# One planned list of steps replaced by another: attention and a gated unit on one core

## The chip, the core and the metric

The kernel runs on one core of a Trainium2 chip. The core has five engines, each with its own queue of instructions that it works through in order: TensorE (PE; its weight loads are PEld), VectorE (DVE), ScalarE (ACT), GpSimd (POOL) and SyncE (SP), which here only issues transfers. ScalarE and GpSimd issue some transfers too. The metric is the time of one execution in microseconds of device time, the median of several runs.

## The reference

For 8 batches of 8 heads, 576 tokens and 64 columns a head, all float32:

```python
kv = np.einsum('bhsd,bhse->bhde', k, v)
out = np.einsum('bhsd,bhde->bhse', q, kv)
rms = np.sqrt(np.mean(out * out, axis=-1, keepdims=True) + 1e-06)
x = out / rms * g_norm              # then heads side by side: (8, 576, 512)
gate_pre = sum over 5 taps of conv_w[tap] * x shifted by 4 - tap tokens
gate = 1 / (1 + np.exp(-gate_pre))
result = (gate * (x @ w_val)) @ w_out
```

w_val, conv_w and w_out come as 512 x 512, 5 x 512 and 512 x 512 arrays of 8-byte floats, which the kernel turns into 4-byte ones by itself.

## The kernel before

The kernel is a list of steps. PLAN (line 19) is a text of 1242 steps, each a name with its arguments and, behind an @, the numbers of the rooms that it takes. The loop at line 882 goes through the list and calls the function of each step, which records its instructions. Every engine's queue therefore holds its instructions in the order of the list, and a step waits where its inputs or its room are not ready; what stands behind it on the same engine waits too. A room is one of a few fixed buffers (line 274): 8 banks of PSUM, 4 of "ot" (output rows), 4 of "gate", 3 of "w64" (staged weights and token sums), 3 of "sq", 3 of "x", one each of k0, k1, v0 and v1 and so on.

For a batch b the steps are these:

- load_half (line 339) loads one half of k or v, 576 KB; load_q (350) loads a pair of heads' rows of q with four transfers into one of three places of qs. All of them are on SP's queue but for a few of batch 0.
- kv_product (467, TensorE, 72 small matmuls) makes k^T v for half of the heads, kv_copy (487, ScalarE) copies it, turn_q (496, VectorE) transposes one load_q.
- raw_pair and raw_tail (566, 569, recorded at line 550) multiply q by kv, for two chunks of 128 tokens or for the last 64. square (582, ScalarE), sums (603, VectorE), powers (612, GpSimd, the root) and normalise (619, ScalarE, eight operations at line 635) make x. For four of the five chunks turn_blocks (659, VectorE) and move_blocks (663, two transfers on SP and two on GpSimd) transpose it, for the last one turn_x and keep_x (644, 650) do; halo (672, GpSimd) shifts the first rows.
- gate_start (677, ScalarE), four gate_taps (683, VectorE, line 685), gate_end (690, ScalarE, the sigmoid at line 692) and gated (708, VectorE, line 710) make one of four blocks of the gate and multiply it in.
- Batches 0 and 1 multiply x by w_val with val_product (694, TensorE) and keep_val. From batch 2 on the product is done in seven smaller ones in place of eight: x_sums (722, VectorE), val_fast (733, TensorE, line 746) and val_keep (750, ScalarE or VectorE).
- Two batches together are an output group i. token_sums (802, VectorE), fast_product (818, TensorE, line 837) and fast_keep (841) multiply by w_out in the same manner, out_product (771, line 784) and keep_out do the last 64 tokens of both. store (865, line 869) issues four transfers of 64 KB on SP's queue, store_last (862) the last rows, two on SP and two on ScalarE.

At the start q of batches 0 and 1 is turned by TensorE (turn_q_rows, 507, and sort_q, 523), and the weights are narrowed: stage_weight (439) loads a quarter of w_val or w_out (512 KB, SP's queue) and narrow_weight has eight parts for it, numbered 0, 5, 6, 4, 7 on VectorE (lines 399, 416, 421, 411, 425) and 1, 2, 3 on ScalarE. Part 4 is the last that reads the staged quarter and so frees its w64 room. val_product reads a column block of w_val after part 7 of it.

The order in the list is a planner's, written out; the kernel holds nothing of the planner. Steps of different batches are woven together: while batch b is multiplied by w_val, batch b + 1 is normalised and the output group before is multiplied by w_out.

Of the kernel before, what the change touches and what calls it, by code (L numbers as in the profile page):

```python
# [22 lines left out]
turn_q_rows 0 3 @ 4; sort_q 0 2; turn_q_rows 0 0 @ 5; sort_q 0 3; start_warm 3 256 @ 6; load_q_rows 1 1;  # L23
sort_q 0 1; load_q_rows 1 0; stage_weight wval 2; kv_product 0 0 @ 7 0; sort_q 0 0; load_half v 1 1;
narrow_weight cw 0 0 @ 0; load_half k 1 1; kv_half 0 0; raw_half 0 3 0 @ 2; narrow_weight cw 0 1;
narrow_weight cw 0 2; kv_product 0 1; stage_weight wval 3; narrow_weight cw 0 3; stage_weight wout 0 @ 1;
narrow_weight cw 0 4; narrow_weight wval 0 0 @ 1; raw_half 0 0 0 @ 3; stage_weight wout 1 @ 2; kv_half 0 1;
narrow_weight cw 0 5 @ 0; narrow_weight cw 0 6 @ 1; raw_half 0 2 0 @ 4; narrow_weight cw 0 7;
narrow_weight wval 0 1; raw_half 0 3 1; narrow_weight wval 0 5 @ 2; raw_half 0 0 1; narrow_weight wval 0 6 @ 3;
square 0 3 @ 0; raw_half 0 4 1 @ 6; square 0 0 @ 1; turn_cw @ 1; sums 0 3 @ 0 0; raw_half 0 2 1;  # L30
narrow_weight wval 0 2; raw_half 0 4 0; powers 0 3; narrow_weight wval 1 0 @ 0; keep_cw; load_half v 1 0;
square 0 2 @ 2; raw_half 0 1 0 @ 5; sums 0 0; square 0 4 @ 0; narrow_weight wval 0 3;
narrow_weight wval 1 5 @ 0; raw_half 0 1 1; sums 0 4; start_warm 1 256 @ 0; narrow_weight wval 1 1;
load_half k 1 0; sums 0 2; square 0 1 @ 1; narrow_weight wval 0 4; powers 0 2; narrow_weight wval 1 2;
sums 0 1; load_half v 2 0 @ 0; turn_q_rows 1 3 @ 7; narrow_weight wval 1 3; normalise 0 3 @ 0;
turn_q_rows 1 0 @ 1; sort_q 1 3 @ 1; narrow_weight wval 0 7; turn_x 0 3 @ 0; load_q 2 2;
narrow_weight wval 2 0 @ 1; turn_q_rows 1 1 @ 2; narrow_weight wval 1 6 @ 1; powers 0 1; keep_x 0 3;
normalise 0 4 @ 1; turn_q_rows 1 4 @ 7; normalise 0 2 @ 2; narrow_weight wval 2 1; turn_x 0 4 @ 6;
narrow_weight wval 1 4; keep_x 0 4; turn_x 0 2 @ 0; narrow_weight wval 2 2; narrow_weight wval 2 5 @ 2;
kv_product 1 1 @ 4 6; narrow_weight wval 1 7; keep_x 0 2; narrow_weight wval 2 3; narrow_weight wval 2 6 @ 3;  # L40
val_product 0 1 1 @ 0; sort_q 1 1; narrow_weight wval 3 0 @ 0; halo 0; normalise 0 0 @ 0; load_half k 2 1 @ 0;
normalise 0 1 @ 1; sort_q 1 4; turn_x 0 0 @ 3; narrow_weight wval 3 5 @ 0; narrow_weight wval 2 4;
turn_x 0 1 @ 2; narrow_weight wval 3 1; stage_weight wout 3 @ 0; val_product 0 0 1 @ 5;
narrow_weight wout 0 5 @ 1; keep_x 0 0; narrow_weight wout 1 5 @ 2; narrow_weight wval 2 7; keep_x 0 1;
narrow_weight wval 3 2; narrow_weight wout 1 6 @ 3; val_product 0 0 0 @ 7; narrow_weight wout 0 0 @ 1;
narrow_weight wval 3 3; narrow_weight wout 0 6 @ 2; gate_start 0 0 @ 0; narrow_weight wval 3 6 @ 1; sort_q 1 0;
narrow_weight wval 3 4; kv_product 1 0; gate_tap 0 0 3; gate_start 0 3 @ 1; narrow_weight wval 3 7;
turn_q_rows 1 2 @ 3; narrow_weight wout 1 0 @ 0; gate_start 0 1 @ 2; val_product 0 3 0 @ 2; gate_tap 0 0 2;
load_q 2 1; kv_copy 1 1; kv_copy 1 0; sort_q 1 2; gate_tap 0 3 3; gate_tap 0 0 1; raw_tail 1 @ 6 1; load_q 2 0;
gate_tap 0 3 2; keep_val 0 0 0; raw_pair 1 3 @ 3 4; keep_val 0 0 1; square 1 4 @ 0; gate_tap 0 1 3;  # L50
keep_val 0 3 0; raw_pair 1 1 @ 5 7; gate_start 0 2 @ 3; gate_tap 0 0 0; square 1 3 @ 2; val_product 0 1 0 @ 2;
sums 1 4 @ 1 1; keep_val 0 1 1; gate_tap 0 1 2; load_half k 2 0 @ 0; square 1 2 @ 1; powers 1 4;
narrow_weight wout 1 1; sums 1 3; load_half v 2 1 @ 0; square 1 1 @ 0; gate_tap 0 1 1; powers 1 3;
val_product 0 2 0 @ 0; narrow_weight wout 1 2; narrow_weight wout 3 5 @ 0; gate_tap 0 2 3; normalise 1 4 @ 2;
sums 1 2; narrow_weight wout 1 3; turn_q 2 2 @ 0; turn_x 1 4 @ 1; normalise 1 3 @ 0; powers 1 2;
# [5 lines left out]
load_half k 3 1 @ 0; narrow_weight wout 0 3; gate_tap 0 3 1; kv_copy 2 0; powers 1 1; normalise 1 0 @ 2;  # L61
val_sums 1; val_product 1 1 1 @ 6; narrow_weight wout 0 4; gate_tap 0 3 0; gate_end 0 0; halo 1; kv_copy 2 1;
# [3 lines left out]
sums 2 0 @ 0 0; val_product 1 0 1 @ 6; narrow_weight wout 2 1; weight_sums 0; keep_x 1 1; powers 2 0;  # L66
load_q 3 0; narrow_weight wout 3 0 @ 0; gate_end 0 2; gated 0 0; square 2 1 @ 2; val_product 1 3 0 @ 1;
gated 0 2; narrow_weight wout 3 1; sums 2 1; square 2 3 @ 0; load_half v 3 1 @ 0; narrow_weight wout 2 5 @ 0;
narrow_weight wout 3 2; turn_q 3 2 @ 1; val_product 1 2 0 @ 0; gate_start 1 2 @ 2; sums 2 3; square 2 2 @ 1;
load_half v 3 0 @ 0; narrow_weight wout 2 6 @ 2; narrow_weight wout 3 3; powers 2 3; load_half k 3 0 @ 0;  # L70
gate_tap 1 2 3; narrow_weight wout 2 2; val_product 1 1 0 @ 2; sums 2 2; keep_val 1 3 0;
narrow_weight wout 2 3; turn_q 3 1; gate_end 0 3; powers 2 2; narrow_weight wout 2 4; val_product 1 2 1 @ 1;
keep_val 1 0 1; keep_val 1 1 0; token_sums 0 0 2 @ 1; keep_val 1 2 0; gate_start 1 0 @ 0;
narrow_weight wout 3 4; normalise 2 3 @ 1; gated 0 3; powers 2 1; val_product 1 0 0 @ 6; turn_q 3 0;
narrow_weight wout 3 7; keep_val 1 2 1; load_q 3 3; normalise 2 2 @ 2; narrow_weight wout 2 7;
fast_product 0 1 0 @ 2; gate_tap 1 0 3; kv_product 3 1 @ 1 0; token_sums 0 0 0 @ 2; fast_keep 0 1 0 @ 3;
load_q 4 0; keep_val 1 0 0; normalise 2 0 @ 0; turn_blocks 2 2; fast_product 0 0 0 @ 5; weight_sums 1;
weight_sums 2; fast_product 0 0 1 @ 7; normalise 2 1 @ 2; turn_blocks 2 3; fast_product 0 0 3; turn_blocks 2 0;
kv_product 3 0; token_sums 0 0 1; fast_keep 0 0 0 @ 0; fast_keep 0 0 1 @ 1; gate_start 1 1 @ 3;
turn_blocks 2 1; raw_tail 2 @ 6 3; val_sums 3; fast_product 0 1 1 @ 4; move_blocks 2 3; square 2 4 @ 2;  # L80
token_sums 0 0 3; move_blocks 2 1; sums 2 4; fast_product 0 1 2; fast_keep 0 1 1 @ 2; gate_tap 1 0 2;
move_blocks 2 0; fast_product 0 0 2; turn_q 3 3; fast_keep 0 1 2; gate_start 1 3 @ 1; fast_product 0 0 5;
gate_tap 1 0 1; kv_copy 3 1; fast_keep 0 0 2; powers 2 4; move_blocks 2 2; kv_copy 3 0; gate_tap 1 3 3;
fast_product 0 1 4; load_half v 4 1 @ 0; weight_sums 3; fast_product 0 0 4; normalise 2 4 @ 1; gate_tap 1 1 3;
raw_pair 3 1 @ 0 1; gate_tap 1 0 0; load_q 4 2; fast_keep 0 0 4; raw_pair 3 3 @ 3 6; gate_tap 1 3 2;
square 3 1 @ 0; fast_keep 0 1 4; fast_product 0 0 6; square 3 3 @ 1; sums 3 1 @ 1 1; square 3 0 @ 2;
fast_keep 0 0 5; fast_product 0 1 6; powers 3 1; load_q 4 1; square 3 2 @ 0; gate_tap 1 2 2; gate_end 1 0;
# [829 lines left out]
```

## Time and profile before

| | |
|---|---|
| median of 3 runs | 299.33 us (298.89 to 300.11) |
| the profiled execution | 300.76 us |
| its span, first to last instruction | 299.0 us |
| granted TensorE clock, mean | 0.996 |
| TensorE matmuls, weight loads | 287.7 us, 225.3 us busy |
| VectorE, ScalarE, GpSimd | 270.1, 198.4, 119.2 us busy |
| transfers | 55.51 MB, mean 186 GB/s |
| instruction queue q8 | 26 packets, 0.43 MB |

The span is the time from the first instruction to the last. "Busy" is the time in which an engine has at least one instruction at work. A row of waits reads: who waited, the line of its instruction, for whom, total us, number of waits, the longest. A row of the chain or of the timeline begins with the start and the length in us. The name behind a DMA wait is that of a transfer that shares the semaphore with the awaited one, which need not be the same transfer. A step's times follow from the trace, because each engine's instructions stand there in the list's order. q8 is taken to bring TensorE's program, which is by far the longest: its packets come all through the span, and 0.43 MB over TensorE's 2 x 3279 instructions are 65 bytes for each.

### The profile page before, as it was taken

To read this page: it belongs to the slowest core of one execution; us is meant where nothing else is said; L and a number is where in the kernel's file an instruction comes from. 1 tells how busy PE (TensorE), PEld (TensorE's weight loads), DVE (VectorE), ACT (ScalarE), POOL (GpSimd) and SP (SyncE) were. 2 spreads that over 40 slices of the span, in tenths; PEclk is the share of its full clock that TensorE was granted. 3 is DMA by queue.
4 is the path that set the end of the run, shared out by engine and by line. 5 is a ranking of instruction groups with operands and counts; after the bars stand their busy time and mean duration, and the time that the engine had idled before them with its cause. 6 is when DMAs were issued, how large, how long until landed. Compare 5 with 4: busy or idle time off the path is not lost.

```text
span 299.0 us, 8649 instructions
## 1 busy us (share of the span) xinstructions
PE 287.7 (96%) x3279; PEld 225.3 (75%) x3279; DVE 270.1 (90%) x483; ACT 198.4 (66%) x621; POOL 119.2 (40%) x131
## 2 busy tenths in 40 slices
PE   7988999999999999899999999999999999999994
PEld 3766787878887868678887757888887588788583
DVE  1699999999999999979999999999999998999812
ACT  1899999999685868664389386757477654614230
POOL 3056054663667049610494287040494072000020
PEclk9999999999999999999999999999999999999998
DMA  7999984787599556976979389654551063130244
GB/s 268 381 389 409 269 246 122 235 256 230 139 235 268 182 152 150 277 181 215 259 171 311 85 202 330 171 148 114 136 146 39 21 147 80 49 94 0 74 121 123
DMA packets 32009, 55.51 MB, mean 186 GB/s; under 512 B 6166, under 2 KB 14358, under 8 KB 31968
## 3 DMA queue, kind: packets, MB, share of 16 engines
q1 hardware_dynamic: 29328, 49.50, 56.2%
q0 software_dynamic: 1760, 3.43, 5.2%
q10 hardware_dynamic: 880, 2.03, 1.9%
q8 instruction: 26, 0.43, 0.6%
q14 instruction: 15, 0.12, 0.1%
HBM read 39.21 MB, written 9.44 MB: 163 GB/s over the span
## 4 chain that ended last, share of the span: by engine, by line
PE 57%; DVE 23%; DMA 7%; ACT 4%; POOL 3%; issue 3%; SPq 2%; DVEq 0%; ACTq 0%
PE bank L746 21%; PE bank L837 19%; DVE gate L685 7%; PE bank L475 4%; PE bank L697 4%; PE bank L550 4%; PE bank L784 4%; DMA qs<-in_q_dram 4%; POOL rt L616 2%; DVE xs L731 2%; DMA k<-in_k_dram 2%; DVE ot L847 2%; DVE ss L606 2%; DVE y L660 1%; PE bank L562 1%
## 5 line engine op out<-in xcount | busy, mean ns | idle before, releaser
L685 DVE SCALAR_TENSOR_TENSOR gate<-xT,cwT,gate 128x576 f32<-128x576 f32 x128 | 100.0, 806 | 0.3
L616 POOL TENSOR_TENSOR rt<-ss,mhalf 128x8 f32<-128x8 f32 (+3 forms) x38 | 71.0, 1887 | 57.2 <-DVE ss L606 56.8
L635 ACT ACTIVATE x<-bank,rt 128x64 f32<-128x64 f32 x252 | 56.5, 398 | 2.8 <-POOL rt L616 2.4
L668 POOL DMA_DIRECT2D xT<-y x48 | 26.6, 559 | 71.7 <-issue 27.8
L837 PE MATMUL bank<-wsum,w 128*128 128x256 f32 x192 | 46.8, 381 | 0.0
L837 PEld LDWEIGHTS bank<-wsum,w 128*128 128x128 f32 x192 | 36.0, 190 | 6.6 <-issue 0.8
L746 PE MATMUL bank<-xs,vsum 128*128 128x288 f32 x144 | 38.2, 409 | 0.2 <-DVE xs L731 0.2
L746 PEld LDWEIGHTS bank<-xs,vsum 128*128 128x128 f32 x144 | 26.9, 190 | 8.4 <-ACT gv L755 0.7
L697 PE MATMUL bank<-xT,wval 128*128 128x288 f32 x128 | 32.8, 409 | 0.0
L837 PE MATMUL bank<-wout,gv 128*128 128x256 f32 x128 | 32.7, 383 | 0.0
L692 ACT ACTIVATE gate<-gate 128x576 f32<-128x576 f32 x32 | 22.5, 712 | 12.7 <-DVE gate L685 12.6
L599 ACT ACTIVATE sq<-bank 128x256 f32<-128x256 f32 (+1 forms) x70 | 22.0, 390 | 11.4 <-PE bank L550 11.4
L697 PEld LDWEIGHTS bank<-xT,wval 128*128 128x128 f32 x128 | 23.7, 190 | 6.3 <-DVE wval L425 0.2
L606 DVE TENSOR_REDUCE ss<-sq 128x8 f32<-128x520 f32 (+1 forms) x40 | 24.9, 628 | 2.2 <-ACT sq L599 1.9
L679 ACT ACTIVATE gate<-xT,cwT 128x576 f32<-128x576 f32 x32 | 25.2, 810 | 2.3 <-DMA xT<-y 1.0
L837 PEld LDWEIGHTS bank<-wout,gv 128*128 128x128 f32 x128 | 23.8, 190 | 3.6
L847 DVE TENSOR_TENSOR ot<-bank,ot 128x256 f32<-128x256 f32 (+1 forms) x32 | 17.1, 546 | 10.3 <-PE bank L837 5.8
L746 PE MATMUL bank<-xT,wval 128*128 128x288 f32 x96 | 25.6, 407 | 0.0
L710 DVE TENSOR_TENSOR gv<-gv,gate 128x576 f32<-128x576 f32 x32 | 23.2, 750 | 0.0
L746 PEld LDWEIGHTS bank<-xT,wval 128*128 128x128 f32 x96 | 17.9, 190 | 4.7 <-issue 0.2
L550 PEld LDWEIGHTS bank<-kv,qT 64*64 64x64 f32 x1008 | 16.5, 135 | 5.1 <-issue 2.5
L475 PEld LDWEIGHTS bank<-v,k 64*64 64x64 f32 x1008 | 16.0, 135 | 5.0 <-issue 2.3
(91 smaller groups left out, 459.6 us busy)
## 6 DMA issues: line engine op xcount, KB each, us to landing
qs<-in_q_dram SPq DMA_DIRECT2D x96, 140.0 KB, 3.8
out_dram<-ot SPq DMA_DIRECT2D x136, 64.0 KB, 1.8
k<-in_k_dram SPq DMA_DIRECT2D x14, 576.0 KB, 5.7
v<-in_v_dram SPq DMA_DIRECT2D x12, 576.0 KB, 5.3
xT<-y SPq DMA_DIRECT2D x48, 64.0 KB, 2.6
xT<-y POOLq DMA_DIRECT2D x48, 64.0 KB, 2.5
y<-in_moe_w_val_dram SPq DMA_DIRECT2D x4, 512.0 KB, 11.5
w<-in_moe_w_out_dram SPq DMA_DIRECT2D x4, 512.0 KB, 9.9
```

Of the source, the lines that this page charges most:

```text
L475: nc.tensor.matmul(st["kvps", b][s][r * D:(r + 1) * D, i], st["k", b, i][rows, r, cols], st["v", b, i][rows, r, cols], start=(j == 0), sto ...
L550: nc.tensor.matmul(st["raw", b, c][r][cols, to * D:(to + 1) * D], st["qT", b][rows, hp, first:first + D], kvs[b % 2][rows, hp, :], start=T ...
L606: nc.vector.reduce_sum(out=st["ss", b][:, FIRST[c]:FIRST[c] + n], in_=st["sq", b, c][:, 0:n], axis=AX.X)
L616: nc.gpsimd.tensor_tensor(out=st["rt", b][:, which], in0=st["ss", b][:, which], in1=mhalf[:, which], op=ALU.pow)
L635: nc.scalar.activation(out=x[:, to * D:(to + 1) * D], in_=raw[:, h * D:(h + 1) * D], func=AF.Copy, scale=root[:, to:to + 1])
L668: (nc.sync if i % 2 else nc.gpsimd).dma_start(out=xTs[b % 2][i * TB:(i + 1) * TB, :, first:first + P], in_=y[a * TB:(a + 1) * TB, i])
L679: nc.scalar.activation(out=gate[:], in_=xTs[b % 2][:, jt, HALO:SX], func=AF.Copy, scale=cwT[:, K - 1, jt:jt + 1])
L685: nc.vector.scalar_tensor_tensor(out=gate[:], in0=xTs[b % 2][:, jt, tap * TB:tap * TB + S], scalar=cwT[:, tap, jt:jt + 1], in1=gate[:], op ...
L697: nc.tensor.matmul(val[:], wval[:, kc, jt * P:(jt + 1) * P], xTs[b % 2][:, kc, HALO + n * SV:HALO + (n + 1) * SV], start=(kc == 0), stop=( ...
L710: nc.vector.tensor_tensor(out=both, in0=both, in1=st["gate", b, jt][:], op=ALU.mult)
L746: nc.tensor.matmul(st[bank, "val", b, mj][:], weights_[:, k], tokens()[:, k], start=(n in (0, 1, 3) and k == 0), stop=(k == NK // 2 - 1), ...
L837: nc.tensor.matmul(st[bank, i, p], tokens()[:, k], weights_[:, k], start=(n < 2 and k == 0), stop=(k == NK // 2 - 1), skip_group_check=True)
```

## The change

Only PLAN changes: the same 1242 steps in another order, with other room numbers where the order asks for it (207 lines in place of 206). No step is added or left out, and no function changes. The new order was planned with a model of the machine in which issues of transfers stand still beside fetches of TensorE's program. Nearly every line of the list differs. Below are the lines with the steps that the prediction speaks of; "..." stands for lines left out.

```diff
-load_q_rows 0 1; load_q_rows 0 0; load_half v 0 0 @ 0; load_half k 0 0 @ 0; start_warm 5 256 @ 0;
-load_half v 0 1 @ 0; load_half k 0 1 @ 0; warm_up; stage_weight wval 0; stage_weight wval 1;
-stage_weight cw 0 @ 0; turn_q_rows 0 1 @ 1; turn_q_rows 0 4 @ 2; turn_q_rows 0 2 @ 3; sort_q 0 4 @ 0;
+load_q_rows 0 1; load_q_rows 0 0; load_half v 0 0 @ 0; load_half k 0 0 @ 0; load_half v 0 1 @ 0;
+load_half k 0 1 @ 0; start_warm 5 256 @ 0; warm_up; stage_weight wval 0; stage_weight wval 1;
+stage_weight cw 0 @ 0; turn_q_rows 0 4 @ 1; turn_q_rows 0 3 @ 2; sort_q 0 4 @ 0; turn_q_rows 0 0 @ 3;
...
-narrow_weight wval 3 4; kv_product 1 0; gate_tap 0 0 3; gate_start 0 3 @ 1; narrow_weight wval 3 7;
-turn_q_rows 1 2 @ 3; narrow_weight wout 1 0 @ 0; gate_start 0 1 @ 2; val_product 0 3 0 @ 2; gate_tap 0 0 2;
+gate_tap 0 0 3; sort_q 1 2; turn_q_rows 1 4 @ 0; narrow_weight wval 3 7; val_product 0 0 0 @ 5; load_q 2 0;
...
+val_product 0 3 0 @ 6; gate_tap 0 1 3; kv_copy 1 1; kv_copy 1 0; load_q 2 1; sort_q 1 0; gate_tap 0 0 1;
...
-val_product 0 3 1 @ 6; narrow_weight wout 1 4; val_sums 0; keep_x 1 4; gate_tap 0 2 2; keep_val 0 2 0;
-turn_x 1 3 @ 1; keep_val 0 1 0; normalise 1 2 @ 1; val_product 0 2 1 @ 0; turn_q 2 1; val_sums 2; turn_q 2 0;
-square 1 0 @ 2; turn_x 1 2 @ 2; narrow_weight wout 0 1; gate_tap 0 2 1; load_q 2 3; kv_product 2 0 @ 3 4;
-keep_x 1 3; sums 1 0; keep_val 0 3 1; keep_x 1 2; gate_tap 0 1 0; kv_product 2 1; powers 1 0;
-narrow_weight wout 0 2; stage_weight wout 2 @ 2; sums 1 1; gate_end 0 1; val_product 1 3 1 @ 1; gate_tap 0 2 0;
...
-turn_q 2 3; normalise 1 1 @ 0; turn_x 1 0 @ 2; narrow_weight wout 3 6 @ 1; load_q 3 2; raw_pair 2 1 @ 3 4;
-narrow_weight wout 0 7; keep_x 1 0; narrow_weight wout 1 7; raw_pair 2 3 @ 7 5; keep_val 1 1 1; square 2 0 @ 1;
-gated 0 1; load_q 3 1; keep_val 1 3 1; turn_x 1 1 @ 2; narrow_weight wout 2 0 @ 1; keep_val 0 2 1;
+keep_val 0 3 0; keep_val 0 2 1; gate_tap 0 2 2; normalise 1 4 @ 2; powers 1 2; narrow_weight wout 1 4;
+normalise 1 3 @ 0; raw_pair 1 1 @ 7 6; turn_q 2 0 @ 0; stage_weight wout 2 @ 1; turn_q 2 2; turn_x 1 4 @ 0;
+load_q 2 3; val_product 0 3 1 @ 2; gate_tap 0 3 0; keep_x 1 4; normalise 1 2 @ 1; gate_tap 0 2 1;
...
+powers 1 1; square 1 0 @ 0; val_product 1 1 1 @ 5; narrow_weight wout 2 0 @ 1; load_half k 3 1 @ 0;
...
+keep_val 0 2 0; turn_q 2 3; keep_val 1 1 1; keep_val 1 0 1; weight_sums 0; normalise 1 0 @ 0; turn_x 1 1 @ 4;
+load_q 3 2; narrow_weight wout 3 0 @ 0; raw_pair 2 3 @ 3 2; narrow_weight wout 3 6 @ 1; val_sums 0;
...
-fast_product 0 2 1 @ 5; sums 4 2; fast_keep 0 3 2; fast_keep 0 3 1 @ 3; gate_tap 2 0 2; move_blocks 3 3;
-fast_product 0 2 4; gate_tap 2 1 1; fast_product 0 3 4; sums 4 3; load_half v 5 1 @ 0; fast_keep 0 2 1 @ 0;
-fast_product 0 3 5; turn_blocks 4 0; normalise 4 1 @ 2; load_q 5 1; powers 4 3; gate_tap 2 2 1;
-fast_product 0 2 5; fast_keep 0 2 4; fast_product 0 2 3; gate_tap 2 2 0; load_q 5 2; fast_keep 0 3 4;
...
-x_sums 3 2 @ 2; load_q 5 0; val_fast 3 0 0 @ 1; fast_keep 0 3 6; normalise 4 2 @ 1; x_sums 3 0 @ 0;
-fast_product 0 2 6; gate_tap 2 0 1; kv_product 5 1 @ 5 0; x_sums 3 1 @ 1; fast_keep 0 2 6; val_keep 3 0 0;
+gate_tap 1 3 1; val_keep 2 0 3; val_fast 2 0 6; gate_tap 1 3 0; val_fast 2 1 6; gated 1 1; load_q 5 1;
...
+square 4 1 @ 1; store 0 8; move_blocks 3 3; sums 4 3 @ 0 0; fast_product 0 3 1 @ 3; sums 4 1;
...
+fast_product 0 3 5; x_sums 3 0 @ 0; halo 3; gate_tap 2 0 1; fast_product 0 2 2; gate_tap 2 2 0;
...
+powers 4 3; gate_tap 2 3 1; gate_end 2 0; val_fast 3 1 3 @ 6; load_half v 5 1 @ 0; fast_keep 0 3 5;
+gate_start 2 1 @ 3; load_half k 5 1 @ 0; x_sums 3 1 @ 1; fast_product 0 2 4; fast_keep 0 2 1 @ 2; store 0 6;
...
+load_q 5 0; square 4 2 @ 2; x_sums 3 2 @ 2; val_keep 3 1 0; fast_product 0 2 6; gated 2 0; val_keep 3 0 2;
...
+gate_end 2 3; kv_product 5 1 @ 0 5; x_sums 3 3 @ 3; gate_start 3 0 @ 1; gated 2 3; raw_tail 4 @ 7 2;
...
-fast_keep 2 0 2; gate_tap 5 3 1; fast_product 2 1 1 @ 4; load_q 7 3; fast_keep 2 1 2; gate_start 5 2 @ 2;
...
-fast_product 1 2 1 @ 1; fast_keep 2 0 5; fast_keep 2 0 4; store 2 0; fast_product 2 1 6; turn_q 7 3;
...
-fast_product 1 3 5; fast_keep 1 2 5; fast_keep 1 3 4; fast_product 1 2 6; gate_tap 5 3 0; fast_product 1 3 6;
...
-val_fast 6 0 0 @ 5; gate_tap 5 1 0; halo 6; val_fast 6 1 2; val_keep 6 0 0; gated 5 3; gate_end 5 0;
...
-move_blocks 7 2; keep_out 2 8 @ 0; fast_product 2 3 1 @ 1; gate_tap 6 3 0; fast_product 2 2 1 @ 0; sums 7 4;
...
-fast_keep 2 3 1 @ 2; halo 7; gate_end 6 3; fast_product 2 2 4; fast_keep 2 3 4; token_sums 2 1 3;
-fast_product 2 3 6; fast_keep 2 2 1 @ 0; gated 6 3; fast_product 2 3 5; fast_keep 2 2 4; fast_keep 2 3 6;
+sums 6 2; turn_q 7 0 @ 1; fast_product 2 0 2; powers 6 2; sums 6 3; load_q 7 3; fast_product 2 1 2;
...
+fast_product 2 0 4; fast_keep 2 1 4; fast_keep 2 0 5; fast_product 2 1 5; normalise 6 2 @ 0; turn_q 7 3;
...
+normalise 7 0 @ 0; val_fast 6 0 0 @ 2; store 1 5; gate_tap 5 3 0; x_sums 6 1 @ 0; val_fast 6 0 1 @ 7;
+val_keep 6 0 0; gate_end 5 3; halo 6; store 1 7; val_fast 6 1 1 @ 0; gate_end 5 0; gated 5 3; val_fast 6 0 2;
...
+gated 6 0; fast_product 2 3 6; val_keep 7 0 0; x_sums 7 2 @ 0; val_fast 7 0 2; gate_tap 6 3 0; gated 6 2;
+val_fast 7 1 1 @ 2; val_keep 7 0 2; gate_end 6 3; val_fast 7 1 0 @ 4; val_keep 7 1 1; gated 6 3;
...
-fast_product 3 3 4; fast_keep 3 3 1 @ 1; fast_product 3 3 5; fast_keep 3 3 4; fast_product 3 3 6; store 3 5;
-fast_keep 3 3 5; store_last 3 6 0; store_last 3 6 1; fast_keep 3 3 6; store_last 3 7 0; store_last 3 7 1
+store_last 3 6 1; store_last 3 6 0; fast_keep 3 3 6; store_last 3 7 1; store_last 3 7 0
```

More of the change, by code (lines that the diff above doesn't have):

```diff
@@ L25 @@
[L25 to L45, printed above, removed]
@@ L51 @@
[L51 to L55, printed above, removed]
@@ L66 @@
[L66 to L86, printed above, removed]
@@ L97 @@
-val_fast 2 1 6; fast_keep 0 1 5; val_fast 2 0 6; turn_q 4 0; val_keep 2 1 6; gate_end 1 3; gated 1 2;
-load_q 4 3; val_fast 2 1 5; val_keep 2 0 6; turn_blocks 3 2; gate_start 2 2 @ 0; kv_product 4 0 @ 7 4;
-val_keep 2 1 3; normalise 3 3 @ 2; gated 1 3; store 0 1; gated 1 1; raw_tail 3 @ 5 1; kv_product 4 1;
-gate_start 2 3 @ 2; turn_blocks 3 1; token_sums 0 1 0 @ 0; square 3 4 @ 2; out_product 0 8 @ 3;
-load_half k 5 0 @ 0; gate_start 2 1 @ 1; turn_q 4 1; kv_copy 4 0; kv_copy 4 1; sums 3 4; token_sums 0 1 1;
```

308 lines of the change are left out of this document (182 added, 126 removed).

## Prediction

> **What bounds the kernel now.** I read the page's busy rows first, then the waits of TensorE and of VectorE, then the chain around the longest TensorE wait, and last the load queue there.
>
> ```profile
> span 299.0 us, 8649 instructions
> PE 287.7 (96%) x3279; PEld 225.3 (75%) x3279; DVE 270.1 (90%) x483; ACT 198.4 (66%) x621; POOL 119.2 (40%) x131
> ```
> ```profile
> PE bank L647 <- DVE x L625: 1.9, 3, 1.1
> PE bank L475 <- DMA qs<-in_q_dram: 1.8, 1, 1.8
> PE bank L463 <- POOL ident masks.py:199: 1.4, 1, 1.4
> PE bank L562 <- ACT kvbd L485: 0.7, 1, 0.7
> PE bank L514 <- DMA qs<-in_q_dram: 0.6, 1, 0.6
> ```
> ```profile
> DVE qT L499 <- DMA qs<-in_q_dram: 0.6, 1, 0.6
> ```
> ```profile
> 117.74 4.83 DMA k<-in_k_dram
> 122.57 0.02 issue
> 122.59 5.05 DMA qs<-in_q_dram
> 127.64 1.28 PE bank L475 x72
> ```
> ```profile
> 117.74 0.54 SPq L347 DMA_DIRECT2D k<-in_k_dram  x1
> 118.38 1.24 SPq L668 DMA_DIRECT2D xT<-y  x2
> 119.67 0.59 SPq L347 DMA_DIRECT2D v<-in_v_dram  x1
> 120.30 10.24 SPq L357 DMA_DIRECT2D qs<-in_q_dram  x12
> ```
>
> TensorE is the bound, and VectorE is close behind. The waits sum to under 7 us on TensorE, nearly all ahead of 60 us but for one of 1.85 us, which ends at 127.64. The chain names a load of q there, but kv_product 5 1 reads k and v: v 5 1 was issued at 119.67 and the trace has it landed 7.84 us later, at 127.51, with eight q transfers queued right behind it. VectorE waits for a load once, 0.64 us at 54.8 to 55.4, in turn_q 2 3; raw_pair 2 3 follows it directly. From 60 us to 125 us VectorE has no idle time of note, and so a wait of either engine moves the rest of the kernel.
>
> **The measure.** Nothing is added or taken away: both plans hold the same 1242 steps, with other places in the list and other rooms. So the sum is one of waits. To see what each wait becomes I give every step the time that it took in the profiled execution (spacing of starts: val_fast 0.97 us, fast_product 0.86, val_product 1.94, kv_product 1.10, raw_pair 1.02, turn_x 0.45, out_product 3.58; VectorE's from their own rows) and add up, per engine, what stands ahead of a step in its queue: "TensorE work ahead", "VectorE work ahead". All TensorE work is 278.8 us, all VectorE work 269.3 us. In the trace VectorE starts a step 10.8 us after its work ahead between 25 and 42 us of it, 11.5 after the 0.64 us wait, 13.5 after the 127.64 wait.
>
> **The 1.85 us of TensorE at 127.64.** Before, between load_half v 5 1 and kv_product 5 1 the list has five fast_products, three val_fasts and a turn_x of a short chunk: 5 x 0.86 + 3 x 0.97 + 0.2 = 7.4 us. It needed 1.85 us more. After, there are three fast_products and eight val_fasts: 10.3 us, and of the q transfers load_q 5 1 and 5 2 now stand ahead of v 5 1, and only k 5 1, a store and load_q 5 0 behind. 10.3 - 7.4 = 2.9 us covers 1.85. What is late next: the shortest distance of any k or v half of batches 2 to 7 was 5.7 us of TensorE work (v 7 0, landed in 4.64) and is now 7.8 (v 3 0); the rows give 5.3 to 5.7 us as the median landing. I count **-1.85**. It lies on the path wholly, since VectorE's clock slipped by the same 1.9 us there.
>
> **The 0.64 us of VectorE at 55.4.** load_q 2 3 had 6.1 us of TensorE work ahead of turn_q 2 3 (two kv_products, two val_products) and now has 10.9 (two val_products and two turn_xs more). Its last transfer took 5.2 us to land. I count **-0.64**: VectorE work up to the end of turn_q 2 3 is 3.0 us less than TensorE work ahead of batch 2's first raw_pair before, 2.9 us after: the two are tied there in both plans, so TensorE gains what VectorE gains.
>
> **A new wait at wout 2.** stage_weight wout 2 moves ahead of load_q 2 3 and takes room 1, which narrow_weight wout 1 4 leaves at 34.3 us of VectorE work; narrow_weight wout 2 0 stands at 41.0 (47.2 before). That is 6.7 us for a transfer of 512 KB, where it had 8.2 us from issue. Bounds: 5.99 us, the landing of wout 2 itself in this trace, and 11.46, the longest of the four; also 7.84, of v 5 1, which like wout 2 now had eight q transfers right behind it. At 5.99 VectorE waits for nothing, at 7.84 1.2 us, at 11.46 4.8 us. I take the middle of the two nearest rows, those of 38 us and later: **+0.6**.
>
> **Gates with no cover.** gate_end (0.71 us on ScalarE) stands between a gate's last tap and gated. In the new queue gates 5 3 and 6 3 have 0.64 and 0.67 us of VectorE work in between, where they had 5.1 and 5.7; the smallest before was 1.0. So VectorE stands still 0.1 to 0.9 us at each (ScalarE free, or one operation of 0.7 us in front of gate_end). What TensorE next takes from behind them, x_sums 6 2 and token_sums 3 0 0, it takes 2.9 and 2.0 us of work later, of which 0.3 are lost to VectorE's later clock. So most of a wait is covered there; I take **+0.2** of the path for all such places.
>
> **Moves that I cost at nothing.** move_blocks of batches 2 to 7, on SP's and GpSimd's queues, shift by -5.4 to +3.6 us of TensorE work; from the last move of a batch to its first val_fast there are 2.6 us or more before and 3.4 after, against a median landing of 2.5 us (TensorE's other work hides them; without it one costs up to 2.5). Stores are nobody's input, but ScalarE waits 7.9 us for the rooms that they leave; ScalarE is 66% busy, which hides that now, and any of it that is not hidden after the change is a loss of the size of its longest, 2.9 us. At the end both lists close with fast_product 3 3 6, its keep and the store_lasts, so the 4.4 us after the last matmul stay.
>
> **A rule weighed.** The change has a model in which issues stand still beside fetches of TensorE's program. The trace shows that they do. Here is the load queue, and the DMA view of the same stretch:
>
> ```profile
> 110.44 1.44 SPq L869 DMA_DIRECT2D out_dram<-ot  x1
> ```
> ```profile
> q8 instruction: 1, 0.02, 5.7%
> ```
> An SP issue takes 0.42 us at the median; this one took 1.44 beside one of the 26 packets of 16 KB of the instruction queue. After 30 us, 16 of the 19 issues over 0.7 us lie beside such a packet, 14.7 us too long together. But neither wait above comes from one of them: the chain to the first runs through ScalarE until 113.6 us, past that packet, and no packet lies beside load_q 2 3. [...]
>
> **Sum.** -1.85 - 0.64 + 0.6 + 0.2 = -1.7 us. The profiled execution took 300.76 us, 1.76 of it outside the span of 299.0; it would be 299.1, with a span of 297.3. The median of the runs shown is 299.33, 1.4 less than the profiled one, so the forecast there is **297.6 us**.
>
> **Rivals.**
> *No change.* One late load is replaced by another of the same kind; the stretched issues, which the new model is for, lay off the path, so the new list is just another list of the same quality. For it: load_q 7 3 has only 6.0 us ahead of turn_q 7 3 (5.2 before), and move_blocks 3 3 7.2 us ahead of x_sums 3 0, where its landings took 4.7 to 5.1 us in this trace and the issues wait for one another. Against: the shortest distances grew for every kind of load. With one more wait of 1.7 us: 299.3.
> *Slower.* The transfer of wout 2 takes what wout 1 and 0 took at 15 to 28 us: 10.5 to 11.46. VectorE, and TensorE behind its wout and taps, stand still 3.9 to 4.8 us at 52 us. Without the +0.6 the sum is -2.3, so this gives 300.9 to 301.8; it decides from a landing of 10.4 us on. Against: the page has the DMA engines at 4 tenths from 45 to 52 us and at 9 from 15 to 28.
> *More.* In the opening TensorE loses 6 us, held by VectorE's narrowing; wval 3 7 now stands 4.6 us of work ahead of val_product 0 3 0 in place of 3.6. If that 1.0 us carries through and wout 2 costs nothing: 299.33 - 1.85 - 0.64 - 1.0 + 0.2 = 296.0. Against: turn_q 2 3 ties both engines again at 50 us as before.
>
> **Chances.** Forecast (296.4 to 298.6) 0.50; no change 0.25; slower 0.15; more 0.10. About 0.5% (1.5 us) is what a measurement of this kernel can tell from no change. Of the forecast, 0.08 lies above 297.8: faster 0.52, same 0.32, slower 0.16 (0.01 for a wait that I don't see). The range reaches to the rivals' times on both sides, 295.4 to 301.0.
>
> **What would show it.** No TensorE wait over 0.5 us at kv_product 5 1; no VectorE wait on q at turn_q 2 3; a wait on the wout transfer of 0 to 1.2 us at L399 near 52 us; waits of VectorE on gate_end under 1 us at gates 5 3 and 6 3; TensorE's waits under 6 us. It is wrong if a TensorE or VectorE wait on a DMA over 1.5 us turns up after 60 us, or if VectorE, not TensorE, carries the chain past 256 us.

## The result, and the profile after

After the change the kernel takes **296.18 us**, the median of five executions (295.98 to 296.36), against 299.33 (298.62 to 300.11) for the kernel before: 3.15 us less, ratio 0.9894 with an interval of 0.9872 to 0.9916. Forecast were 297.6 us. The profiled execution took 296.26 us, 1.8 of it outside the span as before. In three experiments some executions took over 1.5% longer than the fastest of the same kernel; the medians, ratios and intervals given for these experiments leave such executions out.

The page of after, its span and first busy row:

```profile
span 294.5 us, 8675 instructions
PE 285.3 (97%) x3279; PEld 225.3 (77%) x3279; DVE 268.7 (91%) x483; ACT 198.8 (68%) x621; POOL 120.8 (41%) x131
```

All of TensorE's waits behind 60 us, in the waits view of after:

```profile
PE bank L551 <- ACT x L636: 0.3, 1, 0.3
```

This row is at 75 us. From 76 us on the view is empty: TensorE, which waited 1.85 us at kv_product 5 1 before, works to its last matmul without a wait that the profile shows. The same place in the chain of waits, kv_product 5 1 (L476) right behind TensorE's other work:

```profile
129.22 0.86 PE bank L838 x4
130.08 1.94 PE bank L747 x8
132.02 1.21 PE bank L476 x72
```

No load stands in it any more. SP's queue ahead of it, in the timeline:

```profile
114.65 0.48 SPq L348 DMA_DIRECT2D v<-in_v_dram  x1
115.18 1.93 SPq L870 DMA_DIRECT2D out_dram<-ot  x4
117.20 2.96 SPq L358 DMA_DIRECT2D qs<-in_q_dram  x4
120.21 0.42 SPq L348 DMA_DIRECT2D v<-in_v_dram  x1
120.67 0.47 SPq L348 DMA_DIRECT2D k<-in_k_dram  x1
121.78 1.74 SPq L870 DMA_DIRECT2D out_dram<-ot  x4
```

V 5 1 (at 120.21) landed in 3.97 us, 7.8 us ahead of its use; in before it took 7.84 and was 0.14 us ahead. The moves of batch 3 were issued by 114 us, where before they shared this stretch of the queue with the loads (118.38).

To see where the time comes from I use the measure of the prediction: a step's start less the TensorE work ahead of it in the list (277.8 us in all, with the warm-up at 4.87). Its growth over a stage is what TensorE lost there.

| TensorE work ahead | time, about | lost, before | lost, after | less |
|---|---|---|---|---|
| 0 to 72 us | to 81 us | 9.76 | 9.37 | 0.39 |
| 72 to 111 | 81 to 121 | 0.76 | 0.59 | 0.17 |
| 111 to 124 | 121 to 135 | 2.28 | 0.10 | 2.18 |
| 124 to 200 | 135 to 212 | 2.45 | 1.55 | 0.90 |
| 200 to the end | 212 on | 1.63 | 0.81 | 0.82 |

That is 4.46 us, the difference of the two last matmuls (294.6 and 290.2 us). The profile of before is 1.43 us above the median of its times, so 3.15 is to be explained, and not every row holds for the usual execution. The granted clock (mean 0.996 in before, 1.000 in after) is no part of it: in before it is 1.00 up to 296.8 us, 2 us behind the last matmul, and 0.52 only from there on. Two things stand out. TensorE, 1.2 to 1.7 us ahead of before at 24 to 48 us of work, is only 0.4 us ahead at the end of the opening. And behind 135 us, where the prediction had no gain at all, there are 1.7 us.

These 1.7 us can be read step by step in the two traces, as the distance of a step's start from the next one's less the step's usual distance. Four places in before make nearly all of them; after has nothing of the first three and less of the fourth:

- 0.48 us at val_fast 5 0 0 and 5 0 1, behind x_sums 5 0, which waits for a move of batch 5 (0.6 us of VectorE);
- 0.48 us at val_fast 7 0 2, behind VectorE's x_sums of batch 7, though the moves of that batch landed 1.51 us ahead of the first of them;
- 0.31 us at fast_product 3 3 2, behind a copy of ScalarE that had waited 2.9 us for a store to leave its room;
- about 0.45 us at changes to and from steps that use 64 rows of TensorE (kv_product, raw_pair, raw_tail): 9 stretches of them in place of 7, one because kv_product 5 0 now stands in one stretch with kv_product 5 1.

The second of these is the one wait of TensorE that its waits view of before has from 76 us on beside that of the prediction; the third is seen in ScalarE's waits between 287 and 291 us:

```profile
PE bank L746 <- DVE xs L731: 0.2, 1, 0.2
```
```profile
ACT ot L849 <- DMA out_dram<-ot: 2.9, 1, 2.9
```

### The profile page after: what moved, and what is told of

Same layout as the page of the kernel before. It is cut to its first block, busy times and chain, and to the rows that moved or that the text cites. A ratio compares the mean times of both kernels' runs of the same rounds, so it can differ in the third digit from the quotient of the medians.

```text
span 294.5 us, 8675 instructions
## 1 busy us (share of the span) xinstructions
PE 285.3 (97%) x3279; PEld 225.3 (77%) x3279; DVE 268.7 (91%) x483; ACT 198.8 (68%) x621; POOL 120.8 (41%) x131
## 4 chain that ended last, share of the span: by engine, by line
PE 77%; DVE 9%; ACT 8%; DMA 2%; issue 1%; POOL 1%; DVEq 0%; ACTq 0%
PE bank L838 32%; PE bank L747 28%; PE bank L785 5%; PE bank L551 4%; PE bank L476 4%; DVE gate L686 4%; ACT x L636 3%; DMA qs<-in_q_dram 2%; PE bank L563 2%; POOL rt L617 1%; DVE ss L607 1%; DVE ot L422 1%; ACT gv L707 1%; ACT sq L600 1%; PE bank L515 1%
## 5 line engine op out<-in xcount | busy, mean ns | idle before, releaser
L617 POOL TENSOR_TENSOR rt<-ss,mhalf 128x8 f32<-128x8 f32 (+3 forms) x38 | 73.4, 1944 | 81.4 <-DVE ss L607 81.1
L636 ACT ACTIVATE x<-bank,rt 128x64 f32<-128x64 f32 x252 | 55.6, 362 | 4.7 <-POOL rt L617 4.3
L747 PE MATMUL bank<-xs,vsum 128*128 128x288 f32 x144 | 37.2, 407 | 0.0
L854 ACT COPY ot<-bank 128x256 f32<-128x256 f32 x16 | 6.0, 376 | 22.5 <-PE bank L838 22.5
```

The costliest lines, as they stand in the source:

```text
L617: nc.gpsimd.tensor_tensor(out=st["rt", b][:, which], in0=st["ss", b][:, which], in1=mhalf[:, which], op=ALU.pow)
L636: nc.scalar.activation(out=x[:, to * D:(to + 1) * D], in_=raw[:, h * D:(h + 1) * D], func=AF.Copy, scale=root[:, to:to + 1])
L747: nc.tensor.matmul(st[bank, "val", b, mj][:], weights_[:, k], tokens()[:, k], start=(n in (0, 1, 3) and k == 0), stop=(k == NK // 2 - 1), ...
```

## The experiments

Theory at first: the late load at 127 us is the larger part of the gain. Rival: the wait is taken over by the next late thing, and the gain is somewhere else.

**One load moved in the kernel before.**

```diff
-load_half k 5 1 @ 0;
+load_half v 5 1 @ 0; load_half k 5 1 @ 0;
...
-load_half v 5 1 @ 0;
```

> The kernel before with one step moved: load_half v 5 1 stands directly ahead of load_half k 5 1, 3.4 us of TensorE work earlier. Theory (the late load is the larger part of the gain): the 1.85 us wait of TensorE at kv_product 5 1 goes and nothing is late next, so 299.33 - 1.85 = 297.5 us, 297.1 to 298.0. Rival (the time is lost again at another late transfer or in VectorE's queue, and the gain of the new list comes from its opening): 298.9 to 299.6, with a new wait of over 1 us behind 127 us. If the wait varies from run to run and is what spreads the times of the kernel before (298.62 to 300.11), the spread falls below 0.6 us.

Measured: 299.72 us against 299.47 (ratio 1.0003, 0.9981 to 1.0025). The wait of TensorE at kv_product 5 1 is gone, and nothing is won. VectorE's waits between 100 and 145 us in this kernel:

```profile
DVE xs L731 <- DMA qs<-in_q_dram: 1.2, 1, 1.2
```

And SP's queue:

```profile
117.31 0.54 SPq L347 DMA_DIRECT2D v<-in_v_dram  x1
117.89 0.49 SPq L347 DMA_DIRECT2D k<-in_k_dram  x1
118.48 1.29 SPq L668 DMA_DIRECT2D xT<-y  x2
```

The load now stands ahead of move_blocks 3 3, and x_sums 3 2, which needs that move, waits 1.18 us for it. In before the move landed 0.58 us ahead of its use, in after the moves of batch 3 land 1.85 us ahead. The rival held in its first half: the time is lost again at another late transfer (299.72 is just above its 299.6). Its second half, that the gain comes from the opening, is asked below. The times lie closer together, 299.14 to 300.18 in 12 executions against 298.00 to 301.96 in 29 of before, but not below the 0.6 us that were expected if this wait made the spread.

**The transfers behind the load taken away.**

```diff
-load_half k 5 0 @ 0;
+load_half k 5 0 @ 0; load_q 5 1;
...
-move_blocks 3 1;
+move_blocks 3 1; load_q 5 2;
...
-load_q 5 1;
...
-load_q 5 2;
```

> The kernel before with load_q 5 1 and load_q 5 2 moved some 15 us ahead, so that only the four transfers of load_q 5 0 and stores stand behind load_half v 5 1, whose own place in the list stays. Theory A (v 5 1 landed late, 7.84 us after its issue, because eight transfers of q were issued right behind it and shared the DMA engines): it lands in at most 5.7 us, TensorE waits 0 to 0.2 us at kv_product 5 1: 297.5 us. Theory B (7.4 us of work are too few for that load whatever stands behind it): it takes 7 us or more again, a wait of 1 us or more: 298.7 to 299.5.

Measured: 301.04 us; slower, ratio 1.0058 (1.0021 to 1.0095). The profiled execution took 304.86 us. In it v 5 1, with four transfers of q behind it, took 6.57 us, and TensorE waited 2.1 us. The eight transfers of q in front delay what follows on SP's queue: the first store behind them is issued at 115.73 us against 109.81 in before, the load at 124.17 against 119.67, of which 2.0 are a late start of that execution. Theory A falls in this list; B does not follow either, see the run after next.

**Load_q 2 3 earlier in the kernel before.**

```diff
-turn_q 2 1; val_sums 2; turn_q 2 0;
+turn_q 2 0; load_q 2 3; turn_q 2 1; val_sums 2;
...
-load_q 2 3;
```

> The kernel before with turn_q 2 0 ahead of turn_q 2 1 and load_q 2 3 right behind it, so that load_q 2 3 is issued over 1 us earlier. As the prediction has it, VectorE's 0.64 us wait at turn_q 2 3 goes and the end comes as much sooner: 298.7 us. Rival (ScalarE, busy from 15 to 73 us, holds TensorE up to 75 us, so that what VectorE gains at 55 us is lost by 75 us): 299.1 to 299.4, the wait gone all the same.

Measured: 299.41 us against 299.47, ratio 0.9988 (0.9961 to 1.0016): no gain to be seen. VectorE does not wait at turn_q 2 3, but neither does it in the runs e1_v51_up and e4_kv51_early, where that place is as in before (the load landed 1.7 us ahead there). The 0.64 us were one execution's. This trace also shows what TensorE lost at kv_product 5 1 with that place as in before: 0.61 us, against 2.01 in the profile of before; in the first of the two exchanged lists below, which is as before there too, it is 0.18. So the price of the first wait was one of a range, too.

**Load_half v 5 1 late in the kernel after.**

```diff
-load_half v 5 1 @ 0;
...
-load_q 5 0;
+load_half v 5 1 @ 0; load_q 5 0;
```

> The kernel after with one step moved: load_half v 5 1 stands directly ahead of load_q 5 0, 7.5 us of TensorE work ahead of kv_product 5 1, as in the kernel before (7.4), but with four transfers of q behind it in place of eight. Theory A (the transfers behind it made it late): it lands in 4 to 6 us, no wait: 296.2 to 296.5 us. Theory B (the distance alone decides): a wait of 1.0 to 1.9 us comes back: 297.2 to 298.1 us.

Measured: 296.53 us (296.47 to 297.13). It landed in 4.20 us, 4.3 us ahead of its use. The distance of 7.5 us, too short before, is ample here, with a queue in front that is not full. The run before last had the same distance and the same four transfers behind it, and there the load took 6.57 us. So neither of the two decides alone. That the whole stretch of SP's queue does is what remains; it is argued, and no run isolates it.

**Both halves at 105 us, where SP stands still.**

```diff
-load_half k 5 0 @ 0;
+load_half k 5 0 @ 0; load_half k 5 1 @ 0; load_half v 5 1 @ 0;
...
-load_half k 5 1 @ 0;
...
-load_half v 5 1 @ 0;
```

> The kernel before with load_half k 5 1 and v 5 1 moved right behind load_half k 5 0, to 105 us, where SP's queue stands still for 3.3 us; so the moves of batch 3, which shared SP's queue with them, are issued about 1 us sooner. Theory (the two loads and move_blocks 3 3 stand in one busy stretch of SP's queue, 108.5 to 130 us, and what is put first there makes the other late; the wait at 127 us goes only when the stretch gets shorter): no wait of TensorE at kv_product 5 1, none of VectorE at x_sums 3 2, and 0.8 to 2.0 us gained: 297.4 to 298.7 us against 299.4. Rival (other transfers or engines take the time back, so the stretch at 127 us is not where the new list gains): 299.0 to 299.8.

Measured: 299.14 us against 299.63, ratio 0.9994 (0.9974 to 1.0015). The stage at 127 us is clean, lost there are 0.36 us. The waits come back further on; the longest of VectorE between 105 and 200 us, then those of TensorE from 76 us on:

```profile
DVE xs L731 <- DMA qs<-in_q_dram: 1.0, 1, 1.0
```
```profile
PE bank L746 <- DVE xs L731: 0.5, 2, 0.3
PE bank L837 <- ACT ot L851: 0.4, 1, 0.4
PE bank L837 <- ACT ot L849: 0.2, 1, 0.2
```

The first is x_sums 5 0 at 178 us: move_blocks 5 3 landed 4.5 us after its issue, behind it in the queue load_q 7 1 and three loads of batch 7. The landing of a batch's last move against its first x_sums:

| moves of batch | 3 | 5 | 6 | 7 |
|---|---|---|---|---|
| before, us ahead | 0.58 | 0.51 | 0.68 | 1.51 |
| after, us ahead | 1.85 | 3.55 | 1.47 | 2.46 |

With 0.2 to 0.5 us VectorE can in fact have waited, for where it did it starts that much after the landing that releases it (0.22 in the first run's wait, 0.51 for batch 5 in before, in the first, the third and this run). It need not: batch 6 in this run has 0.39 us and no wait. This formed the theory that I kept: the list of before has many places with half a microsecond or less, one wait hides the next, and the new list has room at all of them.

**The two halves of the lists exchanged.** These lists are put together of both; no short diff can show them.

> A list put together of both: all steps that the list of before has ahead of val_fast 2 1 2 (93 us), in the order that the list of after gives them, then the rest as in the list of before; seven rooms differ. It has the opening of after and the remainder of before. Theory (ScalarE holds TensorE up to 75 us in both, so the opening brings next to nothing and the gain lies behind it): 298.9 to 299.5 us. Rival (what TensorE is ahead at 24 to 48 us, 1.6 us, carries through): 297.4 to 298.2 us.

Measured: 300.31 us, ratio 1.0022 (0.9989 to 1.0054), above the theory's range and further above the rival's. The opening of after brings nothing to the rest of before. At 48 us of work TensorE has lost 7.05 us, as in after (6.95), against 8.65; at 72 it is 9.50.

> The counterpart: all steps that the list of after has ahead of val_fast 2 1 2 in the order of before, then the rest as in the list of after; 19 rooms differ. Theory (the gain lies behind the opening): 296.2 to 296.9 us. Rival (the opening brings half of it): 297.5 to 298.3 us.

Measured: 299.26 us, ratio 0.9986 (0.9970 to 1.0002). Neither 296.2 to 296.9 nor a proof of the rival. 2.4 us more than after are lost between 81 and 104 us, at the seam, where engines stand in the order of one list and the rooms of the other. TensorE's waits from 76 to 110 us:

```profile
PE bank L475 <- ACT x L635: 1.2, 1, 1.2
PE bank L746 <- DVE xs L731: 0.5, 2, 0.3
```

Behind 110 us the view is empty, and from 111 us of work on 2.45 us are lost, in after 2.46, although everything runs 2.5 us later. The opening of before had lost 9.42 us at 72 us of work, that of after 9.37. So the two openings end level, and the rest of the new list does not depend on when it begins. That reading is from the trace; the time of a list without the seam stays open.

**Packets of TensorE's program in other places.** 

```diff
+        if n == 5:
+            n = 3
+            for _ in range(64):
+                nc.tensor.matmul(bank[0:TB, 0, 0:TB], ident[:, 0:TB], ident[:, 0:TB], start=True, stop=True)
         for _ in range(n):
```

> The kernel after with two of the five wide warm-up matmuls at the start left out and 64 narrow ones in their place, while TensorE waits for q; they change no result. 62 more matmuls with their weight loads are 124 instructions, about half of a 16 KB packet of TensorE's program, so that every later packet of q8 falls about half a packet interval (some 5 us) elsewhere against the issues on SP. Theory (stretched issues lie off the path): 296.0 to 296.5 us, as many long issues as before the shift, but beside other steps. Rival (the list fits the places of the packets, as the model that planned it has it): the time goes up by 0.7 us or more.

Measured: 298.45 us (297.94 to 299.79), and no answer. In the profiled one (299.60) the narrow matmuls ran to 7.8 us and the first turn_q_rows came at 9.20 us, 2.96 late; that is nearly all of its 3.34 us over the profile of after. And 62 matmuls are 248 instructions, not 124: the timeline of this kernel has two passes for each narrow one (x128 for the 64), and the pages of before and after have a weight load for each pass (3279 and 3279). At the 65 bytes an instruction that the page of before gives, that is 16.1 KB by estimate, about a whole packet (16.4), so the packets lie beside the same steps again. What it does tell: behind 81 us it lost 3.41 us, after 3.04.

Then with 1 wide and 33 narrow ones, in both lists:

> The kernel after with four of the five wide warm-up matmuls at the start left out and 33 narrow ones in their place, which end, by the 52 ns a pass that the run before showed for them, before q has landed; they change no result. 29 matmuls more are 116 instructions of TensorE, a little under half a 16 KB packet of its program, so every later packet of q8 comes some 5 us earlier against the steps. (The run with 64 narrow ones moved the packets by a whole one, which puts them back beside the same steps, and started 3 us late; it told nothing of this.) Theory A (the stretched issues lie off the path wherever they fall): 296.0 to 296.6 us. Theory B (the list has its room where the packets come, as the model that planned it has it): some move or load is late, a wait of TensorE or VectorE on a transfer turns up after 76 us, and the time is 0.7 to 2.5 us longer: 296.9 to 298.7 us.

> The same exchange of warm-up matmuls in the kernel before. Theory A (off the path): within 0.4 us of the kernel before, 299.1 to 299.9. Theory B (a stretched issue beside a move or load that is late already makes part of the waits of before): the time changes by over 0.7 us, either way, with the waits at kv_product 5 1 (0.6 to 2.0 us in the traces so far) and at x_sums 5 0 (0.3 to 1.0 us) larger or gone.

Measured: after with the shift 301.77 us (301.00 to 302.36), before with it 305.91 (305.20 to 307.42), against 299.87 for the kernel before beside them: 5.6 and 6.0 us more than without. The first time is above what either theory had. The second is within theory B's words (a change of over 0.7 us), but most of it comes ahead of 24 us of work, where neither theory had any. TensorE's timeline of the shifted after kernel does not show a late transfer:

```profile
12.49 1.04 PE L480 MATMUL bank<-v,k 64*64 64x64 f32 x54
15.73 0.56 PE L480 MATMUL bank<-v,k 64*64 64x64 f32 x18 [2.21 <-issue]
```

In the middle of kv_product 0 1, whose inputs were there, TensorE stands still for 2.21 us with nothing that it waits for. The DMA view of 13 to 14.5 us:

```profile
q1 hardware_dynamic: 492, 0.54, 110.2%
q8 instruction: 1, 0.02, 4.8%
```

A packet of q8 starts at 13.23 us. The shifted before kernel has the same: packet at 13.14, TensorE still for 1.80 us from 13.98 to 15.78. In before and after that packet comes at 14.85 and 14.29, and no such gap is there. The shifted after kernel has a second, shorter one, 0.46 us in kv_product 7 0 at 196 us, with a packet at 194.04. By 24 us of work the shift costs 3.6 us in after and 3.4 in before. The gap and its end are 2.5 and 2.1 of this. The rest is lost in the 3.5 us behind it, where the granted clock falls to half; the stretch from 16.7 to 20.2 us of the shifted after kernel, the clock being the third number from the end:

```profile
16.70:20.20 3.50, 3.50 (x18) 3.23 (x17) 1.04 (x4) 2.94 (x6) 0.00 (x0) 0.51 1.05 379
```

In the shifted before kernel it is 0.51 from 17.4 to 20.8 us; in after and before it is 1.00 there. From 76 us on the shifted after kernel has no wait of TensorE or VectorE on a load or a move, though 16 of its 17 long issues overlap a packet. So theory A is right about SP's issues, and both theories miss that TensorE itself can stand still beside a packet. That it has run out of program, and that this is no other effect of the changed warm-up, is argued from the two coinciding gaps; no run separates it further. Behind 24 us of work the shift costs about 1.2 us more in after and 1.4 in before. It hurts both lists alike, so there is no sign that the new list is better for fitting the packets.

**ScalarE relieved in the opening of after.**

```diff
+        elif n == 1 and key[0] == "wout":
+            nc.gpsimd.tensor_scalar(
+                out=e, in0=e, scalar1=896, scalar2=1151, op0=ALU.max, op1=ALU.min)
+        elif n == 2 and key[0] == "wout":
+            pass
+        elif n == 3 and key[0] == "wout":
+            nc.scalar.activation(
+                out=e, in_=e, func=AF.Identity, bias=biases[0:rows, 3:4], scale=float(1 << 23))
```

> The kernel after with the exponents of w_out narrowed in two operations in place of three: parts 1 and 2, two ScalarE operations of 0.6 us for each quarter, become one operation of GpSimd that limits the exponent to both ends; part 3 stays on ScalarE with another constant. ScalarE has 5 us less to do between 47 and 71 us. Theory (ScalarE, with no idle time from 50 to 75 us, is what costs TensorE 2.4 us there): 294.4 to 295.7 us. Rival (VectorE, which works without a gap as well, or GpSimd's slower operation in front of powers takes its place): 296.0 to 297.5 us.

Measured: 297.52 us (297.17 to 299.07), 1.3 more than after. The rival held. The table of stages of this kernel, its columns the engines' busy time:

```profile
50.00:60.00 10.00, 10.00 (x203) 8.28 (x195) 10.00 (x20) 7.34 (x29) 9.78 (x8) 1.00 0.89 250
60.00:70.00 10.00, 10.00 (x75) 7.46 (x77) 10.00 (x19) 9.37 (x32) 5.84 (x5) 1.00 0.80 234
```

ScalarE is idle for a quarter of the first stage, VectorE (third) has no gap, and at 60 us of work TensorE has lost 7.84 us in place of 7.97: so ScalarE was not what held it. That VectorE does is argued from its having no gap. GpSimd (fifth) is full in the first stage, its new operation takes 2.1 us, and TensorE pays at raw_tail 2, at 76 us:

```profile
PE bank L559 <- ACT x L644: 0.9, 1, 0.9
```

**SP's queue of before mended in four places.** Beside the edits of the third and the fifth run:

```diff
-load_q 7 1;
-load_half k 7 1 @ 0;
-load_half k 7 0 @ 0;
-load_half v 7 1 @ 0;
-store 1 2;
+store 1 2; load_q 7 1; load_half k 7 1 @ 0; load_half k 7 0 @ 0; load_half v 7 1 @ 0;
...
-store 2 2; sums 7 0; move_blocks 6 2;
+sums 7 0; move_blocks 6 2;
...
-move_blocks 6 3;
+move_blocks 6 3; store 2 2;
```

> The kernel before with its transfers put in better places, and one pair of VectorE steps exchanged for that; the order of TensorE, ScalarE and GpSimd's arithmetic is as before. Load_half k 5 1 and v 5 1 at 105 us and load_q 2 3 earlier, as in the runs before, and beside that load_q 7 1 and the halves k 7 1, k 7 0 and v 7 1 behind store 1 2 (they were issued right behind move_blocks 5 3, whose landing took 4.5 us, and VectorE waited 1.0 us for it at x_sums 5 0), and store 2 2 behind move_blocks 6 3. Theory A (the gain of the new list is a sum of waits on transfers, which SP's order alone can mend): with the waits at 127 us, 176 us and 217 us gone, 297.0 to 298.3 us. Theory B (a transfer that is mended uncovers the next wait, on rooms and on other engines' results, since the engines' own order in the list of before leaves half a microsecond and less in many places): 298.7 to 299.6 us, with waits of TensorE on ScalarE's and VectorE's work in their place, and 5 us or more of TensorE's time lost behind 76 us, where the list of after loses 3.1.

Measured: 303.25 us, ratio 1.0124 (1.0090 to 1.0157), slower than both theories had it. Up to 216 us theory A holds: the waits at 127 and 176 us are gone, and at 200 us of work TensorE has lost 12.77 us, against 15.24 in before, 13.09 in the third run and 14.07 in the fifth, and 11.61 in after. Then one of my own edits undoes it. ScalarE's and TensorE's waits from 205 to 230 us:

```profile
ACT ot L851 <- DMA out_dram<-ot: 5.0, 1, 5.0
```
```profile
PE bank L837 <- ACT ot L851: 3.2, 1, 3.2
```

Store 2 2, put behind the moves, leaves its room so late that ScalarE waits 5.0 us for it, and fast_product 1 3 5 behind that: TensorE loses 5.2 us by 225 us. 3.4 of them are that wait. The other 1.8 are lost behind it, where the granted clock falls to half (third number from the end):

```profile
220.90:224.40 3.50, 3.50 (x10) 2.75 (x9) 3.46 (x6) 1.75 (x10) 3.32 (x5) 0.51 0.00 0
```

Without this stretch the run would be at about 298.1 us (303.25 - 5.2, an estimate). By that estimate SP's order alone could win about 1.1 us (299.14 of before beside this run, less 298.1) of the 3.15. It is no measurement: no run has the four mendings without the late store.

## Why the prediction was right, and where it was not

The sign held. The measured 296.18 us lie below the forecast's own 296.4 to 298.6 and only inside the wide range of 295.4 to 301.0. (The sum of the slower rival goes to 301.8, beyond that range.) The mechanism, waits that go because the list gives them more room, is the right kind, but that the sign came from it is in part luck: each of the two waits that I priced, taken away alone, is worth nothing that can be measured. The size came out at half, because I priced two single waits of one execution and took the rest of the list for equal.

- **-1.85 at kv_product 5 1.** The wait is gone, and the stage lost 2.18 us less. But by itself it is worth nothing that can be measured (first and fifth run: +0.1 and -0.2 us by the ratios). The step that failed in it is "what is late next": I looked for the next late load of k or v and found 7.8 us of distance. Next were the moves of the same batch, on the same queue. The price was also that of one execution (2.01 lost; 0.61 and 0.18 in two others).
- **-0.64 at turn_q 2 3.** Gone, but it was not there in most executions of before either. Its removal in the third run gave 0.1 us by the medians and 0.4 by the ratio, whose interval includes 1.
- **+0.6 at wout 2.** It did not come. The transfer landed in 5.14 us, below the nearest row of before (5.99), and 1.26 us ahead of narrow_weight wout 2 0. I had taken the middle of two rows where the lower one was right.
- **+0.2 at gates 5 3 and 6 3.** VectorE waits there, 0.97 and 0.48 us (0.1 to 0.9 were predicted), but TensorE has no wait behind them: the cover of 2.0 to 2.9 us of work was whole.

```profile
DVE gv L711 <- ACT gate L693: 1.5, 2, 1.0
```

- **Everything behind 135 us costed at nothing.** This is the step that missed most of the gain, 1.7 us in the two profiles. The moves are one part of it: I set 2.6 us of TensorE work against a median landing of 2.5 us and called it hidden. An equality is no cover: in before the moves of batches 3, 5 and 6 landed 0.5 to 0.7 us ahead, and behind those of batch 5 VectorE stood still in before and in the first, third and fifth run. In after they have 1.5 us or more. But that is 0.48 of the 1.7 us. Of the rest, 0.48 is VectorE late for val_fast 7 0 2, though not for a move, 0.31 a room that a store left late, and about 0.45 the changes to 64-row steps. The prediction has no term for the first and the last of these three. The third run's profile (298.21 us), whose list is as before behind 60 us, has 0.29 at val_fast 5 0 0, 0.37 at val_fast 7 0 2, nothing at fast_product 3 3 2 and the same changes, so these sizes are single draws too, but for the changes.
- **Stores.** "Any of it that is not hidden is a loss of the size of its longest, 2.9 us" was the right warning: in the last run ScalarE waited 5.0 us for a store moved back, and TensorE lost 5.2. Yet in before, too, ScalarE's wait of 2.9 us was not all hidden: 0.31 us of it reached TensorE at fast_product 3 3 2.
- **The rule weighed.** That the issues beside packets lie off the path is right for the change: 16 of the 20 long issues of after overlap a packet, 15.1 us too long together (before 16 of 19, 14.7), and TensorE waits for none of it. The new model moved the issues, it did not take the stretches away.
- **The rivals.** "More" has the right time, 296.0, by the wrong way: the 1.0 us of the opening did not carry through, as its own counter-argument said; the openings end level. "Slower" needed a landing of 10.4 us and got half. "No change" was right about single edits and wrong about the list as a whole.
- **The signs to look for.** No wait at kv_product 5 1, none on q at turn_q 2 3, gates under 1 us each, waits of TensorE under 6 us: all came. A wait on wout did not, within the 0 to 1.2 us given.

Not settled: how the 3.15 us divide in the usual execution. In the traces of before and of lists that differ from it by one edit TensorE loses 5.1 to 7.1 us behind 81 us (7.1 in before, 5.9, 5.1 and 6.3 in the first, third and fifth run), in after 3.0 and in the fourth run 3.4. The difference of 2.1 to 4.1 us holds the gain, and no single edit isolates more than 0.5 of it. The places above are read from traces; that taking them away together makes the gain is shown by no list but the new one.

## What to carry to other kernels

When a tuned list of steps has a wait, ask which other inputs of the same stretch are within half a microsecond of being late, on the same queue first: in this kernel a wait that was taken away alone was paid again a few steps on, and the list that gained had room at all of those places at once. Price a wait from several executions where there are any; one profile shows one draw. A store is nobody's input, but its room is.

## What the runs showed of the hardware

- **TensorE stood still beside a packet of q8, taken to be its program.** It did so for 2.21 and 1.80 us in the middle of kv_product 0 1 in the two shifted kernels, when a packet started at 13.23 and 13.14 us in place of 14.29 and 14.85; in the first of them q1 was at 110% of the engines' time from 13 to 14.5 us. Kv_product's 72 matmuls and 72 weight loads take 1.28 us; at 65 bytes each they are 9.4 KB by estimate, more than half a packet of 16.4. In before and after no gap of TensorE lies beside the packet at 14.85 and 14.29 us. If the gap of the two shifted kernels is the packet's, one packet cost them 1.8 to 2.2 us.
- **A standstill can cost more than its length.** Behind those two gaps, and behind the wait of 3.2 us at 217 us in the last run, the granted clock was at half (0.51) for 3.4 to 3.5 us, in which TensorE lost another 1.1 to 1.8 us. Behind the wait of 1.85 us in before it stayed at 1.00 (127.6 to 131.1 us). What sets it off no run here shows.
- **64-row steps cost TensorE's neighbours 0.1 us.** A fast_product takes 0.86 us, but 0.96 as the last ahead of a kv_product or raw_pair, and 0.97 as the first behind one; a val_fast 0.97, 1.06 and 1.07; beside a turn_x nothing is added (0.86 to 0.87). That is 0.1 us a change; what TensorE does in it the traces do not show. Both lists have 22 stretches of 64-row steps, but behind 81 us before has 13 and after 11, so about 0.4 us of the gain are changes that moved ahead of that, where they add nothing to be seen (9.76 us lost up to there in before, 9.37 in after).
- **Spread.** Before took 298.00 to 301.96 us in 29 executions, after 295.98 to 296.36 in five. That this is the scatter of the transfers that the list of before waits for is argued: the same load, v 5 1, took 7.84 us in the profile of before and 6.83 in that of the third run.
